# Loading the second pieces of w1 and w2 through two queues, with a new order for the opening of a fused attention and two-layer product kernel

## The chip, the cores and the metric

The kernel runs on one core of a Trainium2 chip. The metric is the device time of one execution in microseconds (us), the median of several runs. Engines are named as in the profile: PE (TensorE matmul), PEld (its weight loads), DVE (VectorE), ACT (ScalarE), POOL (GpSimd) and SP (SyncE, which here only issues transfers).

## What is computed

Three stages follow each other: attention inside chunks of 64 positions, then a gated product, then a product with a cosine gate.

```python
scores = scale * np.matmul(q_c, k_c.transpose(0, 1, 2, 4, 3))   # 8 x 8 heads, 9 chunks of 64
attn = softmax(scores)
x = (attn @ v_c) as [4608, 512]
h = (x @ w1) * (x @ w2) @ w3          # w1, w2: 512 x 1024, w3: 1024 x 1024
x = h @ w_o                           # 1024 x 512
h = x @ w_in                          # 512 x 2048
out = (h * np.cos(h)) @ w_out         # 2048 x 512
```

All weights arrive as 64-bit floats. q, k and v arrive as 32-bit floats.

## The kernel before

The 4,608 tokens are nine blocks of 512, each of four tiles of 128. For each block: four tiles of attention (`attention`, L699 on), a split of the result into two 16-bit parts (`combined`, L643 on), the products with w1 and w2 (`ab`, seven products in place of eight per 2 x 2 quarter, L975), and the product with w3 @ w_o (`u_of`, L1085 to L1087), stored to HBM. Later each block goes through w_in (`h_of`, L1269) and w_out (`y_of`, L1351 to L1353).

Before block 0 can be multiplied, the opening prepares the weights. Each 64-bit weight piece is scaled on ACT and put together from its two 32-bit words on DVE: L602, then L609, L613, L617 (`decode`, for the 8 pieces of w_o and the 16 of w3), or L833, then L836, L839, L842 (`w12_columns`, for w1 and w2). The product w3 @ w_o is computed on PE in 32 bits (`w3_row`: transposes L915, products L923; a product of the program is two recorded matmuls).

w1 and w2 are treated in two column groups each, in the order w1 group 0, w2 group 0, w1 group 1, w2 group 1 (`w12_columns(g, j)`). Each such set has two pieces of 1 MB, 128 partitions by 8 KB. The first piece (b = 0) is one transfer of all 128 partitions (L815). The second piece (b = 1) is wanted with its halves of the partitions exchanged, so it is two transfers of 512 KB, each to 64 partitions (L818, in a loop over `h`). Then follow, for each set: the squares on ACT (L562), column sums by a product with ones on PE (L850), a column maximum (L853) and a short chain of one-column operations on DVE (L537 to L556), four subtractions (L871), and seven pairs of a high part on ACT (L879) and a low part on DVE (L882). The pieces lie in five places of 8 KB in a region called WG (`raw0_p`), so the first five pieces have a place from the start and the last three must wait until an earlier set is done.

Nothing is issued in the order in which it is written. Each step is recorded with `op(engine, cost, priority, ...)`, and `Plan.order` lays the steps out on a model of the five engines: it starts, on each engine that is free, the step with the lowest priority number whose inputs are there by the model. Transfers are modelled as one stream of `DMA_RATE` bytes per us, where a tile of q, k or v counts `ROWS` times its bytes. Each engine then executes its own steps strictly in that order, so an engine whose next step waits holds up all that stands behind it. The priorities of the opening come from constants at L293: `R0, R1` (rows of w3), `C0, C1` (sets of w1 and w2), `A0, A1` (lead and step of the attention of block 0) and `A2, A3` (the same for the later blocks).

```python
for kk in range(K1):
    w3_row(kk, R0 + R1 * kk)
for g in range(2):
    for j in range(2):
        w12_columns(g, j, C0 + 2 * C1 * g + C1 * j)
...
begin, lead, step = start_ab[bl], (A0, A2)[min(bl, 1)], (A1, A3)[min(bl, 1)]
```

SP issues all transfers. Its transfers take turns on eight semaphores, and each waits until the one eight before it has landed, so at most eight are under way; a second piece of w1 or w2 takes two of the eight.

Of the kernel before, what the change touches and what calls it, by code (L numbers as in the profile page):

```python
# [19 lines left out]
P = 128  # L20
# [5 lines left out]

MM = 0.2155
LAT = {"PE": 0.35, "DVE": 0.4, "ACT": 0.4, "POOL": 0.5, "SP": 2.2}
DMA_RATE = 380e3
ROWS = 2.7  # L30
AHEAD = 5.0
SHARED = 0.8
ISSUE = {"DVE": 0.9, "ACT": 0.88}
# [31 lines left out]
class Plan:  # L65
# [50 lines left out]
    def order(self):  # L116
# [26 lines left out]
        now, done, wakes, order, on_psum = 0.0, 0, [0.0], [], False  # L143
# [12 lines left out]
        while done < len(ops):  # L156
# [3 lines left out]
            now = heapq.heappop(wakes)  # L160
# [7 lines left out]
            for e in ENGINES:  # L168
# [9 lines left out]
                while waiting[e]:  # L178
                    x = heapq.heappop(waiting[e])
                    o, taken, where = ops[x[1]], [], []  # L180
# [19 lines left out]
                if got is None:  # L200
                    continue
                o = got
                o.start, o.eng, o.cost = now, e, o.alts[e]
                if e == "DVE":
                    if not o.psum:
                        o.cost += SHARED * max(0.0, free["POOL"] - now)
# [6 lines left out]
                if o.size:  # L213
                    dma = max(dma, now + o.cost) + o.size / DMA_RATE
                    end = dma
# [18 lines left out]
    def emit(self, split):  # L234

        order = self.order()
        last = {}
        for n, o in enumerate(order):
            for b in o.bufs:
                if b.pool is not None:  # L240
                    for x in b.pool.places:
                        if x[0] == "PS" and x[2] == 2 and b.pool.places[b.place] == x:
                            last[x[1]] = n
        then = {n: i for i, n in last.items()}
        for n, o in enumerate(order):
            o.fn(o.eng) if o.many else o.fn()
            if n in then:
                split(then[n])
        return order
# [6 lines left out]
def fused_kernel(  # L256
# [19 lines left out]
    nc = tc.nc  # L276
    B, H, S, D = q.shape
    NT, DM = out.shape
    F1 = w1.shape[1]
    F2 = w_in.shape[1]  # L280
    CH = 64
# [8 lines left out]
    scale = 1.0 / math.sqrt(D)  # L290
    KB = 1024

    R0, R1, C0, C1, A0, A1, A2, A3, I0, I1, I2, I3, I4, I5, F0, F1, Y0 = 0.9, 10.9, 16.5, 27.6, 60.0, 6, 70.0, 10.6, 240.5, 10.0, 28.1, 510.5, 5.6, 11.6, 8.4, -26.5, 55.8  # L293

    const = ctx.enter_context(tc.tile_pool(name="const", bufs=1))
    sb = ctx.enter_context(tc.tile_pool(name="sb", bufs=1))
# [5 lines left out]
    op = plan.op  # L302
# [134 lines left out]
    at = 95.0  # L437
# [5 lines left out]
    at = start_ab[NB - 1] + 4 * group  # L443
# [9 lines left out]
    with tc.manual_schedule():  # L453
# [168 lines left out]
        def block_of(bl, prio, step):  # L622

            for j in range(TPB):
                i = bl * TPB + j
                vt = vts[i] = Buf(v_p, f"v{i}")
                def f(i=i, vt=vt):
                    dst = vt.ap.rearrange("p (c h d) -> p c h d", c=2, h=HP)
                    for c in range(2):
                        bb, s = divmod(i * P + c * CH, S)  # L630
                        for h2 in range(2):
                            nc.sync.dma_start(
                                dst[h2 * CH : (h2 + 1) * CH, c], v[bb, h2::2, s : s + CH, :].rearrange("h p d -> p h d")
                            )
                op("SP", 2.4, prio + step * j - 8, f, w=[vt], size=ROWS * P * 2 * KB)
            xf[bl] = Buf(xf_p, f"xf{bl}")
# [62 lines left out]
        def attention(i, prio):  # L699
# [5 lines left out]
            for src, b in ((q, qt), (k, kt)):  # L705
                def f(src=src, b=b):
                    dst = b.ap.rearrange("p (h d) -> p h d", h=H)
                    for off, n, bb, s in runs:
                        nc.sync.dma_start(dst[off : off + n], src[bb, :, s : s + n, :].rearrange("h p d -> p h d"))
                op("SP", 0.6, prio - 12, f, w=[b], size=ROWS * P * 2 * KB)  # L710
            qkT = []
# [89 lines left out]
        def w12_columns(g, j, prio):  # L801
# [5 lines left out]
            w = (w1, w2)[j].bitcast(U32)[:, cols].rearrange("(c b p) n -> b p c n", c=2, b=2)  # L807
            for b in range(2):
                raw = raws[b] = Buf(raw0_p, f"raww{j}{g}{b}")
                at = prio + b  # L810

                def f(raw=raw, w=w, b=b):
                    dst = raw.ap.rearrange("p (c n) -> p c n", c=2)
                    if b == 0:
                        nc.sync.dma_start(dst, w[0])  # L815
                    else:
                        for h in range(2):
                            nc.sync.dma_start(dst[h * CH : (h + 1) * CH], w[1, (1 - h) * CH : (2 - h) * CH])  # L818
                op("SP", 0.6 * (1 + b), at - 14, f, w=[raw], size=P * 8 * KB)
            cs = Buf(ps_mm, f"pscs{j}{g}")  # L820
            for b in range(2):
                raw, at = raws[b], prio + b
# [9 lines left out]
                def f(high=high):  # L832
                    nc.scalar.activation(high().bitcast(F32), high().bitcast(F32), AF.Copy, scale=2.0**-112)  # L833
                op("ACT", 1.1, at - 2, f, r=[raw], w=[raw])
                def f(high=high, whole=whole):
                    nc.vector.tensor_scalar(whole(), high(), 3, None, ALU.logical_shift_left)  # L836
                op("DVE", 0.75, at, f, r=[raw], w=keys)
                def f(low=low, whole=whole):
                    nc.vector.scalar_tensor_tensor(whole(), low(), 29, whole(), ALU.logical_shift_right, ALU.bitwise_or)  # L839
# [28 lines left out]
            at = prio + 3  # L868
# [505 lines left out]
# [3 lines that stand above are left out]
# [56 lines left out]
```

## Time and profile before

| | |
|---|---|
| median of 3 runs | 1452.89 us (1451.71 to 1454.46) |
| the profiled execution | 1456.48 us |
| its span, first to last instruction | 1454.7 us |
| PE busy in it | 1413.4 us (97%) |
| DVE, ACT, POOL busy | 992.3, 997.8, 347.1 us |
| mean granted TensorE clock | 0.988 of full speed |

The profiled execution took 1.8 us more than its span, and 3.6 us more than the median of the runs. Busy shares are means over the whole program; the opening is read apart from the rest. PEclk is the granted clock of PE as a share of full speed. The idle time beside an instruction is that of its engine just before it, with what ended it.

### The profile page before, as it was taken

How to read it: one execution, taken by the hardware profiler on the slowest of the kernel's cores; microseconds unless marked ns; L12 is line 12 of the kernel's file. 1: busy time of each engine (PE TensorE's matmuls, PEld its weight loads, DVE VectorE, ACT ScalarE, POOL GpSimd, SP SyncE). 2: the span in 40 equal slices, each digit the busy share in tenths (PEclk: the TensorE clock that was granted, in tenths of full speed). 3: DMA queues.
4: the chain of work that ended last, by engine and by line, in shares of the span. 5: the costliest groups of instructions: out<-in, count | busy, mean ns of one | idle time of the engine just before them, and what ended most of it. 6: DMA issues, size and time to landing. Idle time of an engine off the chain costs nothing.

```text
span 1454.7 us, 28969 instructions
## 1 busy us (share of the span) xinstructions
PE 1413.4 (97%) x11683; PEld 979.5 (67%) x11688; DVE 992.3 (68%) x1587; ACT 997.8 (69%) x2152; POOL 347.1 (24%) x250
## 2 busy tenths in 40 slices
PE   5789999999999999999999999999999999999998
PEld 4346768777777768686876777666666666666644
DVE  8779788468997654578589888757485756454510
ACT  5688777678887676697488888667585756574610
POOL 0000014122653111124145342313141322122100
PEclk8989999999999999999999999999999999999999
DMA  9951383227679222275534443333151333333000
GB/s 313 266 116 44 105 292 84 65 68 221 192 224 264 66 60 66 66 216 180 193 106 174 156 160 144 138 116 145 67 194 67 145 109 117 116 116 116 16 22 29
DMA packets 170454, 194.81 MB, mean 134 GB/s; under 512 B 118992, under 2 KB 133328, under 8 KB 169168
## 3 DMA queue, kind: packets, MB, share of 16 engines
q1 hardware_dynamic: 170320, 192.97, 41.8%
q8 instruction: 91, 1.49, 0.4%
q14 instruction: 43, 0.35, 0.1%
HBM read 162.53 MB, written 30.41 MB: 133 GB/s over the span
## 4 chain that ended last, share of the span: by engine, by line
PE 87%; DVE 5%; ACT 4%; DMA 3%; issue 1%; POOL 0%; ACTq 0%; POOLq 0%; SPq 0%
PE ps L1269 21%; PE ps L975 20%; PE ps L1353 8%; PE ps L1351 8%; PE ps L1352 8%; PE ps L1085 4%; PE ps L1086 4%; PE ps L1087 4%; PE ps L923 2%; PE ps L716 2%; PE ps L779 1%; PE ps L731 1%; DMA u_dram<-TMP 1%; PE ps L764 1%; ACT ATT L748 1%
## 5 line engine op out<-in xcount | busy, mean ns | idle before, releaser
L975 PE MATMUL ps<-XHL,W 128*128 128x256 f16 x3024 | 348.9, 273 | 4.9 <-ACT RES L482 4.7
L1269 PEld LDWEIGHTS <-ATT 128*128 128x128 f16 x3024 | 295.7, 98 | 61.2 <-issue 2.3
L975 PEld LDWEIGHTS <-W 128*128 128x128 f16 x3024 | 293.1, 98 | 45.0 <-issue 5.9
L1312 POOL TENSOR_TENSOR W<-W,RES 128x512 f32<-128x512 f32 x105 | 149.6, 1432 | 411.5 <-ACT RES L1309 405.6
L1278 ACT ACTIVATE W<-ps,smalls 128x512 f32<-128x512 f32 x144 | 97.8, 679 | 114.4 <-PE ps L1269 113.9
L1269 PE MATMUL ps<-XHL,ATT 128*128 128x256 f16 x1392 | 167.8, 273 | 1.1 <-ACT W L1278 0.9
L1284 DVE SCALAR_TENSOR_TENSOR W<-ps,smalls,W 128x512 f32<-128x512 f32 x108 | 80.2, 746 | 101.8 <-PE ps L1269 67.4
L482 ACT ACTIVATE RES<-ps,smalls 128x512 f32<-128x512 f32 x126 | 87.1, 697 | 62.8 <-PE ps L975 58.8
L1300 DVE SCALAR_TENSOR_TENSOR RES<-RES,W 128x512 f32<-128x512 f32 x144 | 109.9, 768 | 22.4 <-ACT RES L1296 21.0
L1010 POOL TENSOR_TENSOR WG<-RES,WG 128x512 f16<-128x512 f32 x44 | 58.0, 1324 | 270.6 <-DMA ATT<-in_v_dram 157.5
L1351 PE MATMUL ps<-CONV,W 128*128 128x512 f16 x320 | 121.4, 379 | 0.0
L1353 PE MATMUL ps<-CONV,W 128*128 128x512 f16 x320 | 121.4, 379 | 0.0
L1352 PE MATMUL ps<-CONV,W 128*128 128x512 f16 x320 | 121.4, 379 | 0.0
L1296 ACT ACTIVATE RES<-W,magic 128x512 f32<-128x512 f32 x144 | 102.5, 716 | 27.1 <-DVE W L1284 25.1
L1309 ACT ACTIVATE RES<-RES,half_pi 128x512 f32<-128x512 f32 x144 | 102.6, 715 | 15.1 <-DVE RES L1306 13.8
L995 DVE SCALAR_TENSOR_TENSOR RES<-ps,smalls,RES 128x512 f32<-128x512 f32 x108 | 79.8, 744 | 45.8 <-ACT RES L482 26.8
L1085 PE MATMUL ps<-WG 128*128 128x512 f16 x288 | 109.4, 380 | 0.0
L1086 PE MATMUL ps<-WG 128*128 128x512 f16 x288 | 109.3, 379 | 0.0
L1087 PE MATMUL ps<-WG 128*128 128x512 f16 x288 | 109.3, 379 | 0.0
L748 ACT ACTIVATE ATT<-ps,SMALL 128x64 f32<-128x64 f32 x288 | 85.8, 327 | 21.4 <-DVE SMALL L743 21.4
L1351 PE MATMUL ps<-CONV,WG 128*128 128x512 f16 x256 | 97.2, 380 | 0.0
L1352 PE MATMUL ps<-CONV,WG 128*128 128x512 f16 x256 | 97.1, 379 | 0.0
(186 smaller groups left out, 2504.9 us busy)
## 6 DMA issues: line engine op xcount, KB each, us to landing
ATT<-win_dram SPq DMA_DIRECT2D x72, 896.0 KB, 5.9
CONV<-in_moe_w_in_dram SPq DMA_DIRECT2D x32, 512.0 KB, 6.8
CONV<-in_moe_w_out_dram SPq DMA_DIRECT2D x32, 512.0 KB, 6.7
ATT<-in_v_dram SPq DMA_DIRECT2D x144, 64.0 KB, 2.5
u_dram<-TMP SPq DMA_DIRECT2D x36, 256.0 KB, 2.7
XHL<-u_dram SPq DMA_DIRECT2D x9, 1024.0 KB, 5.4
out_dram<-TMP SPq DMA_DIRECT2D x36, 256.0 KB, 2.0
ATT<-in_q_dram SPq DMA_DIRECT2D x32, 256.0 KB, 3.7
```

The source lines that it names most:

```text
L975: nc.tensor.matmul(ps.ap[:, p * half : (p + 1) * half], w12[j, g].ap[:, b, w_, c, p * P : (p + 1) * P], t[a].ap[:, c, u_], start=(not more ...
L1085: nc.tensor.matmul(ps.ap, wh.ap[:, kk, 0, ns], g[:, 0], start=(kk == 0), stop=False)
L1086: nc.tensor.matmul(ps.ap, wh.ap[:, kk, 0, ns], g[:, 1], start=False, stop=False)
L1087: nc.tensor.matmul(ps.ap, wh.ap[:, kk, 1, ns], g[:, 0], start=False, stop=(kk == K1 - 1))
L1269: nc.tensor.matmul(ps.ap[:, p * half : (p + 1) * half], wins[p].ap[:, b, k, w_], t[a].ap[:, k, u_], start=(not more and p == 0 and k == 0 ...
L1296: nc.scalar.activation(r.ap, hs.ap, AF.Identity, bias=magic)
L1300: nc.vector.scalar_tensor_tensor(r.ap, r.ap, -MAGIC, hs.ap, ALU.add, ALU.subtract)
L1309: nc.scalar.activation(r.ap, r.ap, AF.Sin, bias=half_pi, scale=-2.0 * math.pi)
L1312: engines[eng].tensor_tensor(out=hs.ap, in0=hs.ap, in1=r.ap, op=ALU.mult)
L1351: nc.tensor.matmul(ps.ap, tg.ap[:, kk, 0, js], wout.ap[:, kk, 0], start=(kk == 0), stop=False)
L1352: nc.tensor.matmul(ps.ap, tg.ap[:, kk, 0, js], wout.ap[:, kk, 1], start=False, stop=False)
L1353: nc.tensor.matmul(ps.ap, tg.ap[:, kk, 1, js], wout.ap[:, kk, 0], start=False, stop=(kk == K2 - 1))
```

## The change

The second piece of each set is still two transfers of 64 partitions, but SP issues the one for partitions 0 to 63 and POOL the one for partitions 64 to 127. SP's modelled cost of it is that of one issue. Nine constants of the opening's priorities are new, and so are two of the three that model transfers; a third, COLD, makes PE's steps 1.15 times as long in the first 120 us of the model.

```diff
-DMA_RATE = 380e3
-ROWS = 2.7
+DMA_RATE = 390e3
+ROWS = 2.4
+COLD = 1.15
...
-                o.start, o.eng, o.cost = now, e, o.alts[e]
+                o.start, o.eng, o.cost = now, e, o.alts[e] * (COLD if e == "PE" and now < 120.0 else 1.0)
...
-    R0, R1, C0, C1, A0, A1, A2, A3, I0, I1, I2, I3, I4, I5, F0, F1, Y0 = 0.9, 10.9, 16.5, 27.6, 60.0, 6, 70.0, 10.6, 240.5, 10.0, 28.1, 510.5, 5.6, 11.6, 8.4, -26.5, 55.8
+    R0, R1, C0, C1, A0, A1, A2, A3, I0, I1, I2, I3, I4, I5, F0, F1, Y0 = -3.6, 11.6, 8.2, 26.1, 68.9, 12.1, 76.2, 11.3, 240.5, 10.0, 28.1, 510.5, 5.6, 11.6, 8.4, -26.5, 55.8
...
-                        for h in range(2):
-                            nc.sync.dma_start(dst[h * CH : (h + 1) * CH], w[1, (1 - h) * CH : (2 - h) * CH])
-                op("SP", 0.6 * (1 + b), at - 14, f, w=[raw], size=P * 8 * KB)
+                        nc.sync.dma_start(dst[:CH], w[1, CH:])
+                        nc.gpsimd.dma_start(dst[CH:], w[1, :CH])
+                op("SP", 0.6, at - 14, f, w=[raw], size=P * 8 * KB)
```

The changed program has one line more ahead of all that matters here, so L815 of before is L816 now, L882 is L883, and so on.

Three places of the order. First POOL's own queue, from its first instruction of the kernel's body on. Before:

```order
masks.py:197 MEMSET ident_90 128x128
masks.py:199 ISA
masks.py:199 AFFINE_SELECT ident_90<-ident_90 128x128
L457 MEMSET half_pi_95 128x1
L460 MEMSET magic_97 128x1
L1010 TENSOR_TENSOR WG_68<-RES_70,WG_68 128x2x256 x4
```

Now:

```order
masks.py:197 MEMSET ident_90 128x128
masks.py:199 ISA
masks.py:199 AFFINE_SELECT ident_90<-ident_90 128x128
L458 MEMSET half_pi_95 128x1
L461 MEMSET magic_97 128x1
L819 DMA WG_68<-in_moe_w1_dram 64x2x1024
L819 DMA WG_68<-in_moe_w2_dram 64x2x1024
L819 DMA WG_68<-in_moe_w1_dram 64x2x1024
L819 DMA WG_68<-in_moe_w2_dram 64x2x1024
L1011 TENSOR_TENSOR WG_68<-RES_70,WG_68 128x2x256 x5
```

The four halves stand together at the head of POOL's queue. The first two go into places that are free from the start and wait for nothing; the third and fourth wait for DVE to be done with an earlier set.

Second, SP's queue around the first piece of w1's group 1 (the third set). RES, XHL and W12 are places of w3 pieces, ATT those of q, k, v. Before:

```order
L598 DMA XHL_72<-in_moe_w3_dram 128x1024
L709 DMA ATT_71<-in_q_dram 128x8x64
L709 DMA ATT_71<-in_k_dram 128x8x64
L815 DMA WG_68<-in_moe_w2_dram 128x2x1024
L598 DMA XHL_72<-in_moe_w3_dram 128x1024
L818 DMA WG_68<-in_moe_w2_dram 64x2x1024 x2
L632 DMA ATT_71<-in_v_dram 64x4x64 x4
L598 DMA XHL_72<-in_moe_w3_dram 128x1024
L598 DMA W12_67<-in_moe_w3_dram 128x1024 x3
L815 DMA WG_68<-in_moe_w1_dram 128x2x1024
L818 DMA WG_68<-in_moe_w1_dram 64x2x1024 x2
L598 DMA W12_67<-in_moe_w3_dram 128x1024 x2
```

Now:

```order
L816 DMA WG_68<-in_moe_w2_dram 128x2x1024
L818 DMA WG_68<-in_moe_w2_dram 64x2x1024
L710 DMA ATT_71<-in_q_dram 128x8x64
L710 DMA ATT_71<-in_k_dram 128x8x64
L599 DMA XHL_72<-in_moe_w3_dram 128x1024 x2
L633 DMA ATT_71<-in_v_dram 64x4x64 x4
L599 DMA XHL_72<-in_moe_w3_dram 128x1024
L599 DMA W12_67<-in_moe_w3_dram 128x1024
L816 DMA WG_68<-in_moe_w1_dram 128x2x1024
L599 DMA W12_67<-in_moe_w3_dram 128x1024 x2
L818 DMA WG_68<-in_moe_w1_dram 64x2x1024
```

Counted from the start of the queue, 14 pieces of w3 stood ahead of that first piece before, and 12 do now; two w3 pieces now stand between it and its set's second piece.

Third, DVE's queue up to the first low part of block 0's operands (L659 before, L660 now). Before:

```order
L836 TENSOR_SCALAR W12_67<-WG_68 128x1024
L839 SCALAR_TENSOR_TENSOR W12_67<-WG_68,W12_67 128x1024
L537 TENSOR_REDUCE smalls_87<-ps_3_76 128x1
L539 TENSOR_SCALAR smalls_87<-smalls_87 128x1
L553 TENSOR_SCALAR smalls_87<-smalls_87 128x1
L554 TENSOR_SCALAR smalls_87<-smalls_87 128x1
L555 TENSOR_SCALAR smalls_87<-smalls_87 128x1
L556 TENSOR_SCALAR smalls_87<-smalls_87 128x1
L663 TENSOR_TENSOR RES_70<-XHL_72 128x512
L871 TENSOR_TENSOR WG_68<-WG_68 128x512 x2
L663 TENSOR_TENSOR XHL_72<-XHL_72 128x2x256
L659 SCALAR_TENSOR_TENSOR XHL_72<-XHL_72,smalls_87 128x2x256
```

Now:

```order
L883 SCALAR_TENSOR_TENSOR W12_67<-WG_68,smalls_87,W12_67 128x512 x7
L538 TENSOR_REDUCE smalls_87<-ps_3_76 128x1
L540 TENSOR_SCALAR smalls_87<-smalls_87 128x1
L554 TENSOR_SCALAR smalls_87<-smalls_87 128x1
L555 TENSOR_SCALAR smalls_87<-smalls_87 128x1
L556 TENSOR_SCALAR smalls_87<-smalls_87 128x1
L557 TENSOR_SCALAR smalls_87<-smalls_87 128x1
L664 TENSOR_TENSOR RES_70<-XHL_72 128x512
L664 TENSOR_TENSOR XHL_72<-XHL_72 128x2x256
L872 TENSOR_TENSOR WG_68<-WG_68 128x512
L570 SCALAR_TENSOR_TENSOR smalls_87<-smalls_87 128x1
L660 SCALAR_TENSOR_TENSOR XHL_72<-XHL_72,smalls_87 128x2x256
```

The seven low parts of the third set stood behind that point and stand ahead of it now. Counted over the whole queue, what is ahead of it grows by 7 of L882, 1 of L842, 2 of L871, 1 of L853 and one chain of six one-column operations. On PE, what is ahead of the first product of `ab` grows by 4 products of L923 (60 in place of 56), 4 transposes of L915, 4 products with ones (L850) and one sum.

## Rows read from the trace of the kernel before

**Rows 1.** Busy time by stretch: us, each engine (instructions), PEclk, DMA share, GB/s.

```profile
0.00:180.00 180.00, 146.79 (x1138) 97.06 (x1144) 144.66 (x277) 129.80 (x321) 3.50 (x10) 0.91 0.61 166
180.00:1400.00 1220.00, 1215.74 (x10313) 859.56 (x10312) 847.64 (x1311) 864.59 (x1827) 343.65 (x240) 1.00 0.41 134
```

**Rows 2.** The same view for four stretches of the opening.

```profile
0.00:62.08 62.08, 41.12 (x150) 24.62 (x152) 53.20 (x88) 36.89 (x63) 0.78 (x8) 0.87 1.00 304
62.08:94.60 32.52, 25.89 (x225) 15.15 (x226) 18.24 (x39) 24.02 (x71) 0.00 (x0) 0.77 0.56 136
94.60:118.80 24.20, 21.24 (x168) 11.81 (x168) 23.31 (x41) 19.53 (x63) 0.00 (x0) 1.00 0.55 104
118.80:172.50 53.70, 51.45 (x531) 41.40 (x530) 43.57 (x103) 42.99 (x116) 1.16 (x1) 0.97 0.18 41
```

**Rows 3.** Timeline, 54 to 73 us: start, us, engine and work, [idle before].

```profile
54.04 1.25 SPq L818 DMA_DIRECT2D WG<-in_moe_w_dram  x2
...
64.43 1.15 ACT L833 ACTIVATE WG<-WG 128x1024 f32<-128x1024 f32 x1 [1.81 <-DMA WG<-in_moe_w_dram]
69.41 1.13 ACT L833 ACTIVATE WG<-WG 128x1024 f32<-128x1024 f32 x1 [2.79 <-DMA WG<-in_moe_w_dram]
...
72.93 0.17 DVE L755 TENSOR_SCALAR SMALL<-SMALL 128x8 f32<-128x8 f32 x1 [5.18 <-ACT ATT L748]
```

**Rows 4.** Timeline, start of the program: POOL, ACT and DVE.

```profile
1.28 0.10 POOL L460 MEMSET magic<- 128x1 f32 x1
...
4.41 0.67 ACT L602 ACTIVATE RES<-RES 128x512 f32<-128x512 f32 x1 [2.40 <-DMA RES<-in_moe_w_out_dram]
7.61 0.69 ACT L602 ACTIVATE RES<-RES 128x512 f32<-128x512 f32 x1 [1.24 <-DMA RES<-in_moe_w_out_dram]
8.88 0.67 ACT L602 ACTIVATE XHL<-XHL 128x512 f32<-128x512 f32 x1 [0.58 <-DMA XHL<-in_moe_w_out_dram]
...
8.70 0.42 DVE L609 TENSOR_SCALAR CONV<-RES 128x512 uint32<-128x512 uint32 x1
10.49 0.42 DVE L609 TENSOR_SCALAR CONV<-XHL 128x512 uint32<-128x512 uint32 x1
```

**Rows 5.** Groups by line, DVE, 0 to 180 us: busy us, mean ns, idle.

```profile
L871 DVE TENSOR_TENSOR WG<-WG 128x512 f32<-128x512 f32 x16 | 10.6, 686 | 0.1
L842 DVE SCALAR_TENSOR_TENSOR WG<-WG,W 128x1024 uint32<-128x1024 uint32 x8 | 9.8, 1223 | 0.2
L853 DVE TENSOR_REDUCE smalls<-ps 128x1 f32<-128x512 f32 x4 | 2.7, 684 | 0.0
L553 DVE TENSOR_SCALAR smalls<-smalls 128x1 uint32<-128x1 uint32 x6 | 0.9, 154 | 0.2
```

**Rows 6.** Timeline, work of the kinds that the change moves, DVE and PE.

```profile
122.83 4.72 DVE L882 SCALAR_TENSOR_TENSOR W<-WG,smalls,W 128x512 f16<-128x512 f32 x7
...
102.64 3.60 PE L923 MATMUL ps<-CONV,RES 128*128 128x512 f32 x8
117.76 0.59 PE L850 MATMUL ps<-TMP,ones 128*128 128x512 bf16 x2
118.33 0.64 PE L915 MATMUL ps<-ident,TMP 128*128 128x128 f32 x4
```

**Rows 7.** Timeline, where block 0's products start, and a later wait of PE.

```profile
118.80 1.47 PE L975 MATMUL ps<-XHL,W 128*128 128x256 f16 x12
...
117.91 0.75 DVE L659 SCALAR_TENSOR_TENSOR XHL<-XHL,smalls 128x512 f16<-128x512 f32 x1
...
145.62 2.72 PE L975 MATMUL ps<-XHL,W 128*128 128x256 f16 x12 [2.15 <-ACT RES L482]
```

**Rows 8.** Timeline, the last piece of w2: buffer freed, issue, arrival.

```profile
89.81 2.08 DVE L882 SCALAR_TENSOR_TENSOR W<-WG,smalls,W 128x512 f16<-128x512 f32 x3 [0.30 <-ACT W L879]
...
96.19 1.25 SPq L818 DMA_DIRECT2D WG<-in_moe_w_dram  x2
...
105.23 1.18 ACT L833 ACTIVATE WG<-WG 128x1024 f32<-128x1024 f32 x1 [2.64 <-DMA WG<-in_moe_w_dram]
```

## The prediction

> **What bounds the kernel now.** I read the busy time by stretch first. From 180 to 1400 us PE is busy 1215.74 of 1220 us at the full granted clock [rows 1]: the body is PE at work, it has 4.3 us of idle time, and the change takes no product away. So the change can only pay in the opening, where PE is idle 33.2 of the first 180 us [rows 1]. The stretches say who holds it up there [rows 2]. Up to 62 us DVE is busy 53.20 of 62.08 us and PE 41.12: DVE, which puts the weights together, is the bound. From 62 to 95 us DVE works only 18.24 of 32.52 us and PE is granted 0.77 of its clock: both wait. From 95 to 119 us DVE is full again (23.31 of 24.20). From 119 us on PE is, with 2.25 us idle in 53.7.
>
> The timeline names the largest hole [rows 3]. ACT takes its steps in order, and the two pieces of w1's group 1 stand ahead of the first tile's exponentials. ACT waits for the first piece until 64.43 and for the second until 69.41 us; the exponentials come after it, and DVE, which divides by their sums, idles 5.18 us until 72.93. The second piece was issued only at 54.04, as two halves.
>
> The same rows show why halves are dear. From the first piece's arrival to the second's it takes 69.41 - 64.43 = 4.98 us for 1 MB, two transfers of 64 partitions [rows 3]. At the start, 512 KB over all 128 partitions come every 8.88 - 7.61 = 1.27 us [rows 4], so 1 MB in 2.54. The same bytes in rows of the same 4 KB take twice as long on half of the partitions.
>
> The place where opening and body meet: DVE starts the first low part of block 0's operands at 117.91 us, and PE starts the first of the block's products at 118.80 [rows 7]. From there on PE has enough work. So what counts is when that point comes, less the PE work already done by then.
>
> **The change, part by part**, positive for slower.
>
> *1. Work moved ahead of that point: +3.5 us.* DVE does more before it: seven L882 in a row, 4.72 us [rows 6]; one L842, 1.22; two L871, 1.37; one L853, 0.68; six one-column operations of 0.15, 0.90 [rows 5]: 8.9 us. PE also does more before it, which it need not do later: 3.60 for the products of L923, 0.64 for four transposes, 2 x 0.59 for four products with ones [rows 6]: 5.4 us (one small sum is left out). DVE is the bound up to that point, so the start comes 8.9 later with 5.4 more done: 3.5 lost. It can't be much else, as both counts come from the order.
>
> *2. POOL's first two halves: +1.6 us, between 0 and +4.6.* They wait for nothing, and POOL is through with its constants at 1.38 us [rows 4], so 1 MB is asked for while w_o's first pieces are on their way. SP's own halves go out where they stood, tens of us later for the second set, so these two pairs do not run together. 1 MB at the pace of the rows is 2.54 us. I let it land beside the third and fourth piece, since POOL asks after SP's first loads. The fourth then lands at 8.88 + 2.54 = 11.42, is scaled by 12.09 (0.67 for the scaling), and DVE, which began it at 10.49, is 1.6 us late; later pieces have more room. At best POOL's transfers move after w_o's: 0. At worst they take the 4.98 us of two halves and the third piece waits for all of it: 7.61 + 4.98 + 0.69 = 13.28 against DVE's start at 8.70 [rows 4], 4.6 late.
>
> *3. The hole at 64 to 73 us: -4.1 us, between -5.2 and -1.6.* Two w3 pieces fewer stand ahead of w1's group 1: its first piece comes 2 x 1.27 = 2.5 us earlier. Its second now has two w3 pieces ahead (2.5) and one half on SP's queue (2.5, half of 4.98) where it had two (4.98): also 2.5 earlier. ACT and DVE come 1.6 later (term 2). Of DVE's 5.18, 5.2 - 2.5 - 1.6 = 1.1 is left. Below, the hole closes; above, the transfer comes no earlier and only the 1.6 is saved. Next late is then ACT itself, with the exponentials.
>
> *4. DVE's other waits from 62 to 95 us: -2.0 us, between -9.1 and +5.2.* They are 32.52 - 18.24 - 5.18 = 9.1 us [rows 2, 3], many short ones on ACT and PE in the attention of the first tiles. Every engine's order is new there, and no row shows the new meetings. They can all go (-9.1), or one more hole like the largest can open (+5.2 [rows 3]). No row is nearer to one end, so I take the middle, -2.0.
>
> *5. After the point, and in the body: 0, between -4 and +4.* PE's 2.15 us wait at 145.62 on ACT [rows 7] comes while ACT makes seven high parts in a row; in the new order seven still stand between two of its releases from PSUM, now those of the last set. The body's orders change with A2 and A3; its idle time is 4.3 us [rows 1] and PE hides the rest. I give each about 2 us to either side.
>
> POOL's four issues cost nothing: POOL has nothing else before the block's products. If that cover were gone, its first product step would wait behind the fourth half. SP saves four issues and four of its places among eight; that is inside term 3.
>
> **Sum:** 3.5 + 1.6 - 4.1 - 2.0 + 0 = -1.0 us. The profiled execution took 1456.48 us, 3.6 above the median of the runs; I take the difference over to the median: 1452.89 - 1.0 = 1451.9 us. 0.2% is 2.9 us, about what a measurement of this kernel tells from no change.
>
> The Trainium skill, SBUF — State Buffer, section "Can I just issue two DMAs to hit both halves?", speaks against the change: transfers to partitions from 0 and from 64 are said to serialize, with 6% gained by running them together, whichever engine issues them. The 4.98 us for two halves on one queue agrees with it [rows 3], and no run here shows two queues yet. It is the second rival below.
>
> **Rivals.**
> *Faster: the waits of 62 to 95 us give way.* If the two halves move together on two queues, the third set comes in time, the hole closes (-5.2), half of DVE's other waits go (-4.6), and with the last set done sooner PE's 2.15 us wait goes too (-2.2). Sum 3.5 + 1.6 - 5.2 - 4.6 - 2.2 = -6.9: 1446.0 us. For it: the idle time is there, and 8.9 us of the moved DVE work depends on no attention, so it can fill holes. Against it: in an in-order queue it fills them only where the order happens to put it, and the first two pairs don't run together.
>
> *Serial halves.* A pair takes 4.98 us whatever queue it is on. By the skill's rule above this is what happens. Then the second piece of w1's group 1 has two w3 pieces ahead and a full 4.98 behind them, lands at 69.4 as before, and term 3 is only -1.6: 3.5 + 1.6 - 1.6 - 2.0 = +1.5, 1454.4 us.
>
> *Slower: a new wait at w2's last piece.* On ACT it now stands right after the second tile's exponentials and ahead of the third's. Its place comes free when the second set's low parts end, 89.81 + 2.08 = 91.9 us; SP issued it only at 96.19, 4.3 us later, and it landed at 105.23 [rows 8]. If SP's half is again 4.3 us behind, ACT stands still for that long with the exponentials, PE's transposes and DVE's divisions behind it: -1.0 + 4.3 = +3.3, 1456.2 us, and more if term 2 goes to its end. It decides once that half lands after ACT is done with the second tile's exponentials. Before, ACT's wait there was 2.64 us.
>
> **Chances.** My forecast 0.40, of which 0.30 lies within 0.2% and 0.05 on each side; faster rival 0.32; serial halves 0.10 (0.08 within, 0.02 slower); new wait 0.18. So faster 0.37, same 0.38, slower 0.25. The faster rival reaches to 1445, and the slower one, with term 2 at +4.6 in place of +1.6, to 1459; I take 1445 to 1459.
>
> **What would show it.** In the new profile: POOL's two first halves issued near 1.4 us and ACT's scaling of the fourth w_o piece near 11.4 (term 2); ACT's wait for w1's second piece of group 1 ending near 67 us and DVE's idle before its first division near 1 us (term 3); DVE busy over 18 of the 32 us from 62 on (term 4); the first product of `ab` near 118.8 + 8.9 + 1.6 - 4.1 - 2.0 = 123 us (term 1). The forecast is wrong if that product starts before 119 us or after 127, or if PE's idle time from 180 us on differs from 4.3 us by more than 2.

## The result, and the profile after

| | before | after |
|---|---|---|
| median of 6 runs | 1452.99 us (1451.71 to 1454.46) | 1463.84 us (1461.21 to 1465.21) |
| the profiled execution | 1456.48 us | 1465.21 us |
| its span | 1454.7 us | 1463.4 us |
| PE busy, idle in the span | 1413.4, 41.3 us | 1416.3, 47.1 us |

The change makes the kernel slower: the ratio after to before is 1.0071, 95% interval 1.0058 to 1.0084, or 10.9 us between the medians. 1451.9 us was forecast, and the range ended at 1459. The two traces are of single executions, 3.5 and 1.4 us above these medians, so their spans are 8.7 us apart and not 10.9.

The busy time by stretch of the changed kernel has the same columns as [rows 1]: us, each engine (instructions), PEclk, DMA share, GB/s.

```profile
120.00:140.00 20.00, 15.68 (x83) 8.34 (x83) 18.38 (x48) 14.98 (x28) 0.00 (x0) 0.83 0.06 13
...
0.00:180.00 180.00, 141.91 (x1094) 93.05 (x1100) 139.48 (x271) 126.91 (x316) 5.61 (x14) 0.90 0.57 155
180.00:1400.00 1220.00, 1214.98 (x10317) 859.97 (x10316) 852.45 (x1304) 872.18 (x1838) 353.19 (x246) 1.00 0.42 135
```

The body has 5.0 us of idle PE against 4.3 [rows 1]. In the opening PE idles 38.1 us against 33.2, and from 120 to 140 us, where it was busy 19.90 of 20 us in the kernel before, it works 15.68 at 0.83 of its clock.

The timeline of the changed kernel's start answers to [rows 4]:

```profile
1.53 1.35 POOL L819 DMA_DIRECT2D WG<-in_moe_w_dram  x2
...
5.70 0.69 ACT L603 ACTIVATE RES<-RES 128x512 f32<-128x512 f32 x1 [0.61 <-DMA RES<-in_moe_w_out_dram]
10.60 0.67 ACT L603 ACTIVATE RES<-RES 128x512 f32<-128x512 f32 x1 [4.21 <-DMA RES<-in_moe_w_out_dram]
14.75 0.67 ACT L603 ACTIVATE XHL<-XHL 128x512 f32<-128x512 f32 x1 [3.48 <-DMA XHL<-in_moe_w_out_dram]
...
15.45 0.43 DVE L610 TENSOR_SCALAR CONV<-XHL 128x512 uint32<-128x512 uint32 x1 [2.27 <-ACT XHL L603]
```

POOL's first two halves hold back the third and fourth piece of w_o. DVE begins the fourth at 15.45 in place of 10.49: 5.0 us late.

The timeline at w1's group 1 and the first tile answers to [rows 3]:

```profile
60.98 1.16 ACT L834 ACTIVATE WG<-WG 128x1024 f32<-128x1024 f32 x1 [0.82 <-DMA WG<-in_moe_w_dram]
68.31 1.15 ACT L834 ACTIVATE WG<-WG 128x1024 f32<-128x1024 f32 x1 [1.59 <-DMA WG<-in_moe_w_dram]
69.35 0.30 ACT L749 ACTIVATE ATT<-ps,SMALL 128x64 f32<-128x64 f32 x1
...
71.83 0.17 DVE L756 TENSOR_SCALAR SMALL<-SMALL 128x8 f32<-128x8 f32 x1 [2.81 <-ACT ATT L749]
...
72.88 6.75 PE L924 MATMUL ps<-CONV,RES 128*128 128x512 f32 x8 [3.83 <-ACT RES L479]
80.80 0.69 PE L780 MATMUL ps<-ATT 64*64 64x64 f32 x32 [0.29 <-ACT ATT L479]
```

The same place before:

```profile
74.50 1.12 PE L764 MATMUL ps<-ident,ATT 128*128 128x128 f32 x4 [4.36 <-ACT ATT L478]
77.65 1.13 PE L779 MATMUL ps<-ATT 64*64 64x64 f32 x32
...
79.16 6.13 PE L923 MATMUL ps<-CONV,RES 128*128 128x512 f32 x8
```

The first piece comes 3.45 us earlier than before, the second 1.1. DVE's wait before the first division shrinks from 5.18 to 2.81 us. But on PE eight products of w3 (L924) now stand ahead of the first tile's transposes, and the copy on ACT (L479) that they need stands behind the exponentials. PE waits 3.83 us for it (4.36 before, for the transposes' own copy), and the eight products take 6.75 us at 0.54 of the clock, where such a group takes 3.60 at the full clock [rows 6]. So the first tile's P times V (the product of its probabilities with v) comes at 80.80, and before at 77.65, where the eight products followed it. A low clock there is not new: before, they took 6.13 us.

The timeline from the second tile to the first product of `ab` answers to [rows 7, 8]:

```profile
93.00 1.14 ACT L834 ACTIVATE WG<-WG 128x1024 f32<-128x1024 f32 x1 [2.66 <-DMA WG<-in_moe_w_dram]
...
98.22 0.43 DVE L610 TENSOR_SCALAR RES<-W 128x512 uint32<-128x512 uint32 x1 [7.32 <-PE ps L916]
...
124.35 0.69 PE L780 MATMUL ps<-ATT 64*64 64x64 f32 x32 [2.03 <-ACT ATT L479]
127.79 1.11 PE L916 MATMUL ps<-ident,TMP 128*128 128x128 f32 x4 [2.15 <-DVE smalls L538]
128.99 6.01 PE L924 MATMUL ps<-CONV,RES 128*128 128x512 f32 x8
135.40 1.47 PE L976 MATMUL ps<-XHL,W 128*128 128x256 f16 x12
...
130.53 0.75 DVE L660 SCALAR_TENSOR_TENSOR XHL<-XHL,smalls 128x512 f16<-128x512 f32 x1
```

DVE has a new hole of 7.32 us. Its first low part of block 0 comes at 130.53 (117.91 before), the first product at 135.40 (118.80 before): 16.6 us later, with 5.4 us more of PE's work done, so 11.2 us are lost by then. That is more than the 8.7 us between the spans: after it the changed kernel gains. Busy time by stretch from there on, before and then now:

```profile
118.80:180.00 61.20, 58.55 (x600) 45.49 (x599) 49.91 (x111) 49.36 (x128) 2.72 (x2) 0.97 0.27 68
```

```profile
140.00:160.00 20.00, 20.00 (x241) 17.48 (x243) 14.41 (x38) 16.94 (x55) 1.16 (x1) 1.00 0.24 54
```

Before, PE idled 2.65 us between the first product of `ab` and 180 us. Now it does not wait at all there. DVE's busy time up to its first low part, in both kernels (the rows of before have 53.12 us up to 62), tells how the 12.6 us on DVE came:

```profile
62.00:117.91 55.91, 46.32 (x384) 26.17 (x386) 40.77 (x79) 42.79 (x131) 0.00 (x0) 0.86 0.56 125
```

```profile
0.00:62.00 62.00, 39.94 (x138) 24.05 (x140) 49.96 (x83) 34.03 (x56) 2.71 (x11) 0.83 1.02 294
...
62.00:130.53 68.53, 52.55 (x410) 29.08 (x413) 51.91 (x102) 52.28 (x150) 0.58 (x1) 0.90 0.43 110
```

DVE works 101.87 us in place of 93.89 (8.0 more), idles 12.04 in place of 8.88 up to 62 us (3.2 more), and 16.62 in place of 15.14 after it (1.5 more).

### The profile page after: what moved, and what is told of

It reads as the page before. It is cut to its first block, busy times and chain, and to the rows that moved or that the text cites. A ratio compares the mean times of both kernels' runs of the same rounds, so it can differ in the third digit from the quotient of the medians.

```text
span 1463.4 us, 28969 instructions
## 1 busy us (share of the span) xinstructions
PE 1416.3 (97%) x11683; PEld 979.7 (67%) x11688; DVE 991.9 (68%) x1574; ACT 1003.2 (69%) x2159; POOL 358.8 (25%) x260
## 4 chain that ended last, share of the span: by engine, by line
PE 84%; DMA 8%; DVE 4%; ACT 3%; issue 1%; SPq 0%; ACTq 0%; DVEq 0%
PE ps L1270 22%; PE ps L976 19%; PE ps L1354 8%; PE ps L1353 8%; PE ps L1352 8%; PE ps L1086 4%; PE ps L1088 4%; PE ps L1087 4%; DMA WG<-in_moe_w_dram 3%; DMA CONV<-in_moe_w_out_dram 2%; PE ps L924 2%; PE ps L717 2%; PE ps L780 1%; PE ps L732 1%; DMA XHL<-in_moe_w_out_dram 1%; DMA CONV<-in_moe_w_in_dram 1%
## 5 line engine op out<-in xcount | busy, mean ns | idle before, releaser
L1313 POOL TENSOR_TENSOR W<-W,RES 128x512 f32<-128x512 f32 x109 | 157.2, 1449 | 440.8 <-ACT RES L1310 420.5
L1270 PE MATMUL ps<-XHL,ATT 128*128 128x256 f16 x1344 | 162.3, 273 | 1.9 <-DMA ATT<-win_dram 1.6
L1011 POOL TENSOR_TENSOR WG<-RES,WG 128x512 f16<-128x512 f32 x50 | 63.7, 1277 | 285.8 <-ACT WG L479 285.6
L1301 DVE SCALAR_TENSOR_TENSOR RES<-RES,W 128x512 f32<-128x512 f32 x144 | 113.9, 795 | 22.6 <-ACT RES L1297 21.9
```

The costliest lines, as they stand in the source:

```text
L1270: nc.tensor.matmul(ps.ap[:, p * half : (p + 1) * half], wins[p].ap[:, b, k, w_], t[a].ap[:, k, u_], start=(not more and p == 0 and k == 0 ...
L1301: nc.vector.scalar_tensor_tensor(r.ap, r.ap, -MAGIC, hs.ap, ALU.add, ALU.subtract)
L1313: engines[eng].tensor_tensor(out=hs.ap, in0=hs.ap, in1=r.ap, op=ALU.mult)
```

## The experiments

The ratio of each run is to the kernel before on the same chip, with its 95% interval; 0.001 is 1.45 us. The changed kernel stands at 1.0071.

**Is it the split of the loads?** Four kernels: the changed one with all halves on SP (e1), the old order with POOL's halves (e2), the changed one with group 0's halves on SP (e3), and one that makes POOL wait for an earlier piece (e4). PE, DVE and ACT keep their order in all.

```diff
 e1:
-                        nc.gpsimd.dma_start(dst[CH:], w[1, :CH])
+                        nc.sync.dma_start(dst[CH:], w[1, :CH])
 e2, in the kernel before:
-                        for h in range(2):
-                            nc.sync.dma_start(dst[h * CH : (h + 1) * CH], w[1, (1 - h) * CH : (2 - h) * CH])
+                        nc.sync.dma_start(dst[:CH], w[1, CH:])
+                        nc.gpsimd.dma_start(dst[CH:], w[1, :CH])
 e3:
+                        (nc.gpsimd if g else nc.sync).dma_start(dst[CH:], w[1, :CH])
 e4, ahead of POOL's transfer (loaded: the pieces of w_o and w3 that SP has asked for so far):
+                        if g == 0:
+                            nc.gpsimd.tensor_copy(tiny, loaded[-4].ap[:, 0, 0:1])
```

> The changed kernel with POOL's halves put back on SP's queue; PE, DVE and ACT keep the changed kernel's order. Theory A (POOL's two early halves hold back w_o by 5 us and that is carried to the end, the other 6 us are the new order's): the fourth w_o piece is scaled near 9 us again instead of 14.75, the first product of ab starts 3 to 5 us before 135.4, and the time is 1458 to 1460 us. Rival B (the order alone makes all of it, the late start is taken up by later waits): 1463 to 1465 us. Rival C (the two queues alone make all of it): 1452 to 1454 us.

> The kernel before with only the split: second halves on POOL, order of PE, DVE and ACT untouched. Theory A: DVE's first steps come 5 us later, the hole at 64 to 73 us shrinks by 2 to 3, the time is 1455 to 1458 us. Rival B (order alone): 1450 to 1454 us. Rival C (queues alone): 1462 to 1465 us.

> The changed kernel, but the two early halves (group 0) back on SP, the two late ones (group 1) still on POOL. Theory A: the w_o pieces come as in the kernel before, 1457 to 1459 us, no more than 2 us quicker than with all on SP. Rival B: 1463 to 1465. Rival C': if the late pairs on two queues are what costs, this stays at 1463 or more while all on SP is quicker.

> The changed kernel with all four halves on POOL, but POOL's first two held until an earlier piece of SP's queue has landed (POOL copies one word of it per partition), so that they run beside SP's halves. Theory A: as group 0 on SP, 1457 to 1459 us, and the first pair lands in under 4 us if two queues move two halves together, in about 5 if they take turns. Rival B: 1463 to 1465 us.

Measured: e1 1462.12 us, 1.0055 (1.0042 to 1.0068); e2 1452.88, 1.0001 (0.9991 to 1.0011); e3 1465.01, 1.0079 (1.0064 to 1.0094); e4 1464.94, 1.0074 (1.0060 to 1.0088). Rival B holds in the main: the order makes the loss, and in the old order the split costs nothing. In e2 the fourth piece is scaled at 14.80, as late as in the changed kernel, and `ab` still starts at 115.40. The 5 us are real and are taken up by later waits. In e4 the early pairs did not run side by side after all: POOL's halves went out at 16.05 and 28.70 us, SP's at 11.54 and 33.05.

One thing is left over. With all halves on SP, e1 is 2.9 us quicker than e3, as rival C' has it (the late pairs on two queues cost). Their traces don't show that as its cause: in e3 the late pieces of w1 and w2 come no later (67.69 and 91.36 us, against 68.02 and 92.24 in e1), and `ab` starts 0.4 us earlier. The difference of their spans is idle time of PE from 180 to 1400 us (6.28 against 3.28 us), where no half is loaded. In e4 that idle time is 9.6 us, and there `ab` starts 5.0 us earlier than in the changed kernel without any gain. So in this order the body can take back what the opening gives; why stays open.

What the two queues do to a pair was to be seen at w2's last piece. Timeline of e1, both halves on SP, then of the changed kernel:

```profile
84.02 0.61 SPq L818 DMA_DIRECT2D WG<-in_moe_w_dram  x1
84.67 0.62 SPq L819 DMA_DIRECT2D WG<-in_moe_w_dram  x1
...
92.24 1.10 ACT L834 ACTIVATE WG<-WG 128x1024 f32<-128x1024 f32 x1 [3.58 <-DMA WG<-in_moe_w_dram]
```

```profile
85.71 0.59 SPq L818 DMA_DIRECT2D WG<-in_moe_w_dram  x1
...
85.98 0.58 POOL L819 DMA_DIRECT2D WG<-in_moe_w_dram  x1 [30.50 <-DMA ATT<-in_v_dram]
```

From the first issue to ACT's start it is 8.2 us on one queue and 7.3 on two. But the other eight kernels that issue this pair on two queues within 0.3 us, and in which ACT waits for it, need 6.9 (e4) to 8.4 us (v7). For the pair before it, w1's of group 1, 13.7 us pass on one queue (e1) and on two (e3, the changed kernel). No gain of the second queue shows. The Trainium skill, SBUF — State Buffer, section "Can I just issue two DMAs to hit both halves?", says that transfers to the two halves of the partitions serialize and gives 6% for running them together. These pairs agree with it: a gain of that size would lie within what they scatter.

**Is it DVE's hole and the work moved ahead?** The runs named v and b7 leave the plan as it is and move single steps of it (by their number) ahead of another step, each behind all that it reads. PE's order is untouched in all.

```diff
 v2 (plan.own is 2 KB of RES, unused there, for the w3 piece of L610 at 98.22):
+    order = shifted(order, [295, 297, 299, 302, 311], 294)
+    for b in {id(b): b for o in order for b in o.bufs if b.name == "w3_7_0"}.values():
+        b.pool, b.place = plan.own, 0
 v3:
+    order = shifted(order, [381, 383], 366)
 v4:
+    order = shifted(order, [361, 364, 368, 370, 373, 377, 379], 421)
 v5: the lines of v4, then those of v2
 v6 (v4, and ACT's seven high parts):
+    order = shifted(order, [357, 358, 360, 363, 369, 372, 375, 361, 364, 368, 370, 373, 377, 379], 421)
```

> The changed kernel, but the w3 piece whose decoding DVE waits 7.32 us for gets its own 2 KB, and five DVE steps of w1's group 1 (5.5 us) go ahead of the third tile's maximum, so that the hole at 91 to 98 us is filled. Theory D (all of the loss is ahead of the first product of ab, and DVE's hole there is on its path): DVE comes to its first low part 4.5 to 5.5 us earlier than 130.5, ab starts 4 to 5 us before 135.4, the time is 1458 to 1460 us. Rival E (PE and ACT hold the opening up anyway, the hole only moves): 1462 to 1465 us.

> The changed kernel, but DVE reads the small sums (PE's bank) after two of the seven low parts of L883 instead of after all seven. The theory on the join: PE's wait of 2.15 us at 127.79 goes, its eight products of L924 run before DVE is done with block 0's first low part, ab starts near 131.4 in place of 135.4, and the time is 1459 to 1461 us. Rival: these products must be made anyway and PE only waits later, 1463 to 1465 us.

> The changed kernel, but the seven low parts of w1's group 1 (4.72 us of DVE) stand after block 0's low parts instead of ahead of them, as they did in the kernel before. Theory (work moved ahead of the point is paid in full): DVE's first low part of block 0 near 125.8, ab near 130.3 instead of 135.4, 1458 to 1460 us. Rival (PE is the bound at the join, or the seven are waited for afterwards): over 1462 us.

> Both edits of v2 and v4. If hole and moved work are separate causes, the gains add: 9 to 10 us, 1453 to 1455 us, about the kernel before. If they are one cause seen twice: 1458 to 1460 us.

> As v4, and ACT's seven high parts of w1's group 1 go behind block 0's operands too, so that ACT's copy of the fourth tile's transposed probabilities no longer stands behind four of them. Theory F (the fourth tile's attention, through ACT, sets when ab starts, not DVE's work): that copy at 121 to 122 us in place of 124.06, P times V at 122 to 123 in place of 124.68, ab at 128 to 131 in place of 135.1, and 1461 to 1465 us, 4 to 8 below v4. Rival (PE's own queue of w3 products sets it): ab stays at 134 to 136 and the time above 1466.

Measured: v2 1465.55 us, 1.0093 (1.0076 to 1.0109); v3 1462.50, 1.0075 (1.0060 to 1.0089); v4 1469.37, 1.0115 (1.0093 to 1.0138); v5 1466.41, 1.0102 (1.0085 to 1.0119); v6 1464.95, 1.0093 (1.0080 to 1.0106). None is faster than the changed kernel. My theory D and that of the join fell. Busy time by stretch and timeline of v2, then PE at the join in v3:

```profile
100.00:120.00 20.00, 18.85 (x129) 10.27 (x126) 13.41 (x24) 14.73 (x54) 0.00 (x0) 1.00 0.28 64
```

```profile
135.26 1.47 PE L976 MATMUL ps<-XHL,W 128*128 128x256 f16 x12
```

```profile
128.89 5.48 PE L924 MATMUL ps<-CONV,RES 128*128 128x512 f32 x8 [2.73 <-ACT RES L479]
```

The hole is filled (DVE is busy 29.37 us from 62 to 100, against 22.96), and DVE then idles from 100 on instead: 13.41 busy against 18.80. `ab` starts where it did. In v3 PE's wait for DVE at the join is gone, and it waits for ACT's copy in its place, so that the eight products start at 128.89 where they started at 128.99. So DVE is not what bounds this stretch in the new order; the tiles' attention on PE and ACT is. In v6, where ACT's high parts moved too, the product that opens `ab` did come 6.4 us earlier, as theory F has it: 7.8 us after the fourth tile's P times V, in place of 11.1. PE then waited 3.58 us for a small sum behind the seven parts that had been moved, and the time shows no gain:

```profile
128.96 1.47 PE L976 MATMUL ps<-XHL,W 128*128 128x256 f16 x12
...
139.37 0.90 PE L717 MATMUL ps<-ident,ATT 128*128 128x128 f32 x3 [3.58 <-DVE smalls L538]
```

**Which constants?** Three plans made anew, and r3's with e3's line. (Eight of the opening's priorities changed, R0 to A3; the nine told above were a miscount.)

```diff
 r8, changed kernel:  A1 = 12.1 -> 6
 r2, kernel before:   A0, A1 = 60.0, 6 -> 68.9, 12.1
 r3, changed kernel:  DMA_RATE = 390e3 -> 380e3, ROWS = 2.4 -> 2.7, COLD = 1.15 -> 1.0
 s3:                  r3, with e3's line
```

> The changed kernel with one constant set back: A1, the step between the priorities of block 0's four tiles, 6 in place of 12.1; the order is planned anew. Theory F: the fourth tile's P times V comes over 8 us earlier than 124.35, ab starts at 120 to 126, the time is 1453 to 1458 us. Rival (the sets' and w3's priorities or the rates make it): ab stays above 130 and the time above 1461.

> The kernel before with only A0 and A1 of the change (68.9 and 12.1): the four tiles of block 0 spread out, all else old, halves on SP. Theory F: the fourth tile's P times V 6 us or more later than 111.56, ab later than 118.8 by 3 to 8 us, 1455 to 1460 us. Rival: no change, 1451 to 1454.

> The changed kernel with the planner's old rates (380e3, rows at 2.7, no dearer cold products), new priorities kept. If the priorities make the loss: 1459 to 1466 us. If the rates do: 1451 to 1455 us.

> The kernel with the old rates and new priorities, with the two early halves on SP's queue again. If the 5 us by which the early halves hold back w_o are carried to the end in this order: 1447 to 1449 us. If they are taken up by later waits, as in the old and the changed order: 1450 to 1453 us.

Measured: r8 1457.92 us, 1.0051 (1.0037 to 1.0065); r2 1451.48, 0.9997 (0.9986 to 1.0009); r3 1452.18, 1.0004 (0.9995 to 1.0013); s3 1451.50, 0.9996 (0.9986 to 1.0006). With the new priorities and the split, but the old rates, the loss is gone: 0.0067, or 9.7 us, hang on the three numbers with which the planner models transfers and early products. Which of them stays open: no plan with one alone was run. With the old step of the tiles under the new rates (r8), `ab` starts at 122.40 and some 3 us come back, though the intervals of r8 and the changed kernel overlap by a little. Its plan also has the exponentials ahead of w1's second scaling, so the step's own share isn't told apart. In the old order the new step costs nothing (r2), so it isn't the cause by itself.

Timeline of r3, first tile and start of `ab`, and its body:

```profile
64.92 0.31 ACT L749 ACTIVATE ATT<-ps,SMALL 128x64 f32<-128x64 f32 x1 [0.18 <-DVE SMALL L744]
...
67.25 0.62 ACT L479 COPY RES<-ps 128x512 f32<-128x512 f32 x1
67.72 1.21 ACT L834 ACTIVATE WG<-WG 128x1024 f32<-128x1024 f32 x1
...
67.92 3.70 PE L924 MATMUL ps<-CONV,RES 128*128 128x512 f32 x8 [1.15 <-ACT RES L479]
73.38 0.69 PE L780 MATMUL ps<-ATT 64*64 64x64 f32 x32 [0.89 <-ACT ATT L479]
128.46 1.47 PE L976 MATMUL ps<-XHL,W 128*128 128x256 f16 x12
```

```profile
180.00:1400.00 1220.00, 1218.47 (x10295) 860.42 (x10293) 846.09 (x1305) 862.71 (x1821) 350.72 (x245) 1.00 0.41 135
```

Here the exponentials and the copy behind them stand ahead of the two scalings. ACT does them while the loads are under way, PE waits 1.15 us in place of 3.83 and keeps its clock, and the first tile's P times V comes at 73.38, not 80.80. That lead of 7.4 us is 6.9 at the first product of `ab`. 3.5 us more come in the body (1.5 us of idle PE against 5.0; kernels with the changed kernel's order have 3.2 to 9.6 us there). PE's own order is not the cause: up to `ab`, r3 and the changed kernel have the same 558 recorded matmuls in the same order. What differs ahead of it is the order on DVE, ACT and SP.

**Is it the scalings ahead of the exponentials?** ACT's two scalings moved behind them in the changed kernel (v7) and in the kernel before (b7), ahead of them in r3 (v8).

```diff
 v7:
+    order = shifted(order, [175, 200], 213)
 v8, in r3:
+    order = shifted(order, [202, 208], 190)
 b7, in the kernel before:
+    order = shifted(order, [195, 203], 224)
```

> The changed kernel with one edit in ACT's order alone: its two scalings of w1's group 1, which wait for the loads until 60.98 and 68.31 us, go behind the first tile's exponentials and the copy after them. Theory G (the waits for these loads sit ahead of the first tile's exponentials and hold back every tile after it): the exponentials start at 66 to 67 us in place of 69.35, the first tile's P times V at 74 to 76 in place of 80.80, all later tiles and the first product of ab 4 to 6 us earlier than 135.4, 1457 to 1460 us. Rival (the order behind that place makes the loss): ab within 1.5 us of 135.4 and 1462 to 1465 us.

> The kernel with the old rates and new priorities (r3_old_rates, 1452.2) with the opposite edit: the same two scalings put ahead of the first tile's exponentials, where the changed kernel has them. Theory G: the exponentials start near 70 us in place of 64.92, ab at 132 to 135 in place of 128.46, 1456 to 1459 us. Rival: 1451 to 1454 us.

> The kernel before with the same edit as v7: the two scalings behind the first tile's exponentials and three copies. Theory G: the exponentials start near 66 us in place of 70.44, DVE's wait of 5.18 us goes, and the kernel takes 1448 to 1451 us, less than both kernels. Rival (the wait only moves, as the filled hole did): 1451 to 1454 us.

Measured: v7 1465.35 us, 1.0094 (1.0078 to 1.0111); v8 1457.19, 1.0044 (1.0027 to 1.0061); b7 1450.28, 0.9988 (0.9976 to 1.0000). Put in, the order costs r3 0.0040, 5.8 us, as theory G says. With the 3.5 us of the body (v8's body is r3's, 1.6 us of idle PE) that makes 9.3 of the 9.7 us between r3 and the changed kernel. Taken out of the kernel before, which has the exponentials behind the scalings too, it gives some 2 us, at the edge of the interval. In v8's timeline PE waits 3.91 us again, the first tile's P times V is at 77.06 and `ab` at 131.00:

```profile
70.55 5.35 PE L924 MATMUL ps<-CONV,RES 128*128 128x512 f32 x8 [3.91 <-ACT RES L479]
77.06 0.69 PE L780 MATMUL ps<-ATT 64*64 64x64 f32 x32 [0.29 <-ACT ATT L479]
...
131.00 1.47 PE L976 MATMUL ps<-XHL,W 128*128 128x256 f16 x12
```

But taken out of the changed kernel (v7) it gives nothing. Timeline of v7:

```profile
66.62 0.69 ACT L603 ACTIVATE W<-W 128x512 f32<-128x512 f32 x1 [2.13 <-DMA W<-in_moe_w_dram]
67.20 0.29 ACT L749 ACTIVATE ATT<-ps,SMALL 128x64 f32<-128x64 f32 x1
...
70.94 0.65 ACT L603 ACTIVATE W<-W 128x512 f32<-128x512 f32 x1 [1.29 <-DMA W<-in_moe_w_dram]
...
72.12 5.37 PE L924 MATMUL ps<-CONV,RES 128*128 128x512 f32 x8 [4.68 <-ACT RES L479]
78.65 0.69 PE L780 MATMUL ps<-ATT 64*64 64x64 f32 x32 [0.29 <-ACT ATT L479]
...
135.41 1.47 PE L976 MATMUL ps<-XHL,W 128*128 128x256 f16 x12
```

The exponentials start 2.15 us earlier, but PE gains nothing that can be told from scatter. The nine kernels with ACT's steps in the changed kernel's order up to here (with it, e1, e3, e4 and v2 to v6) have the first tile's P times V at 76.83 to 81.31, v7 has it at 78.65, and v9 and v10, with the same edit, at 80.48 and 81.31. What holds PE now is the next steps in ACT's queue. Scalings of w3 pieces (L603) stand ahead of the exponentials and of the copy that PE needs, and they wait for their own loads, 2.13 and 1.29 us. PE waits 4.68 us for the copy, in place of 3.83. In r3's order no scaling stands between the exponentials and the copy, and those ahead of them did not wait. No run moved these scalings too, so this is read from the traces and not shown by an edit.

**Do the waits stand in series?** v9 is v7 with ACT's scaling of w2's last piece (at 93.00 us in the changed kernel) moved behind the second tile's copies; v10 has, besides, v2's filled hole, and DVE's small sums and ACT's copy of the fourth tile ahead of the high and low parts.

```diff
 v9:
+    order = shifted(order, [271], 289)
+    order = shifted(order, [175, 200], 213)
 v10, v9 and v2's lines, and ahead of them:
+    order = shifted(order, [381, 383], 366)
+    order = shifted(order, [357, 358, 360, 361, 363, 364], 370)
```

> The changed kernel with v7's edit and ACT's scaling of w2's last piece (wait of 2.66 us until 93.00, ahead of the copy of the second tile's transposed probabilities) put behind that tile's copies. Theory H (the waits stand in series, each edit alone only hands its gain to the next wait): the second tile's P times V at 91 to 93 in place of 96.47, ab 2 to 4 us before 135.4, 1459 to 1462 us. Rival (PE's own queue sets the pace from 86 us on): ab within 1 us of 135.4, 1463 to 1466.

> The changed kernel with the edits of v9, the filled hole of v2, and at the join DVE's small sums and ACT's copy of the fourth tile's transposed probabilities ahead of w1's group 1's high and low parts. PE's order is untouched. Theory H: the gains that none of the edits had alone come together, ab at 124 to 129 and 1454 to 1459 us. Rival (PE's order itself, w3's products between the tiles, makes the loss): ab at 131 or later and 1461 us or more.

Measured: v9 1459.32 us, 1.0051 (1.0037 to 1.0065); v10 1463.35, 1.0076 (1.0063 to 1.0090). In v9 the second tile's P times V follows 13.98 us after the first's, where it takes 14.83 to 16.05 in v7 and in the nine kernels with that scaling in its old place (15.67 in the changed one). `ab` is at 132.07, 3.3 us earlier than in the changed kernel, but e1, e3 and e4 have it at 130.38 to 133.30 without the edit:

```profile
80.48 0.69 PE L780 MATMUL ps<-ATT 64*64 64x64 f32 x32 [0.29 <-ACT ATT L479]
94.46 0.69 PE L780 MATMUL ps<-ATT 64*64 64x64 f32 x32 [0.88 <-ACT ATT L479]
...
132.07 1.47 PE L976 MATMUL ps<-XHL,W 128*128 128x256 f16 x12
```

With w1's and w2's scalings out of the tiles' way some 3 us come back (0.0020, though the two intervals overlap by a little) that neither v7 nor any other edit to ACT or DVE had. v10 missed. PE comes earlier to its last eight products before `ab`, but ACT's copy for them still stands behind seven high parts, so PE waits 5.34 us and starts them at 129.11 (128.99 in the changed kernel):

```profile
129.11 6.01 PE L924 MATMUL ps<-CONV,RES 128*128 128x512 f32 x8 [5.34 <-ACT RES L479]
```

So v10 doesn't tell whether all waits together cover the loss. That stays open. Its rival, PE's own order, fits v10's numbers (`ab` at 135.53 us) but falls by r3, which has that order and is as fast as the kernel before.

## Why the prediction was wrong

The view of where it would be decided was right: the body gave 0.7 us more idle time, and the loss arises ahead of the first product of `ab`. By the prediction's own sign, that product starting after 127 us, it was wrong: it starts at 135.40. The terms, as forecast and as they came between the two traces:

| term | forecast | came |
|---|---|---|
| 1, moved work (DVE more, PE's part less) | 8.9 - 5.4 = +3.5 | 8.0 - 5.4 = +2.6 |
| 2, POOL's first halves (DVE's idle time up to 62 us) | +1.6 | +3.2 |
| 3 and 4, DVE's waits from 62 us on | -6.1 | +1.5 |
| from DVE's first low part to `ab`, 0.89 to 4.87 us | none | +4.0 |
| 5, after that point | 0 | -2.5 |
| sum | -1.0 | +8.7 (10.9 by the medians) |

**Term 4 is the step that failed first.** It took the middle between "all waits go" and "one more hole", because no row was nearer to one end, although every engine's order was new. One more hole did open, 7.32 us, longer than the 5.18 on which the upper end was set. With term 3 the sum was off by 7.6 us.

**Term 3 was half right.** The pieces came 3.45 and 1.1 us earlier where 2.5 was forecast for both, and DVE's wait fell to 2.81 us in place of 1.1. What the step left out is what else stands behind those scalings on ACT, the copy that PE's eight products need, and that these products now stand ahead of the first tile's transposes: the first division comes 1.1 us earlier than before, the first tile's P times V 3.15 us later.

**The frame "DVE is the bound up to that point" failed**, and with it the way in which the terms were added. v2, v4 and v5 take DVE's waits and moved work away and gain nothing. The kernel r3 has the same seven low parts ahead of the point, starts `ab` 9.7 us later than before, and is as fast as before. For the same reason the start of `ab` was taken as DVE's first low part plus 0.9 us. In the new order PE has eight products ahead of it that wait for DVE's small sum behind the seven low parts (2.15 us) or, with that wait gone, for ACT's copy (2.73 us in v3), and then run at the lower clock (6.01 us); 4.0 us had no term at all.

**Term 2 was sized too low and mattered little.** 5.0 us at the fourth w_o piece is past the upper end of 4.6, but e1, e3 and e2 show that it is worth 0 to 2.3 us at the end.

**Term 5** kept PE's wait of 2.15 us after the start of `ab`. That wait went (2.65 us less idle time up to 180 us), and the body took 0.7 us back.

**The rivals.** "Slower: a new wait at w2's last piece" named a place that counts, though not its price: the wait is 2.66 us, as before (2.64), and moving the scaling brings the second tile 0.9 us or more closer to the first (v9). "Serial halves" is what the pairs do, as far as these runs tell (6.9 to 8.4 us on two queues, 8.2 on one), and it did not decide: e1 and e2 put the loss on the order. "Faster" saw the idle time of 62 to 95 us rightly as usable: in r3 DVE is busy 30.40 of the 38 us from 62 to 100, against 22.96. It was an order that could use it, and the changed kernel's is not.

The range left out such a loss because the ends of the terms were not taken together: terms 2 and 4 at their upper ends alone would have given 1462.1.

## What to carry to other kernels

In an in-order queue a step that waits for a load should not stand ahead of a short chain that other engines wait for: look, for every new order, at which load waits stand ahead of which releases (v8: 5.8 us). The rates with which a planner models transfers count only through the order that comes out: between r3 and the changed kernel two near-equal sets of rates are 9.7 us apart. Waits in series hide each other, so an edit at one of them that brings nothing does not clear it: look at which step of the same queue waits in its place. And before a lead of 2 us in one trace is called the edit's, look at how far the same step scatters between kernels that don't differ there.

## What was not expected of the hardware

POOL's two halves, asked for at 1.53 us, slowed all loads on their way: from 5.70 to 14.75 us 265 GB/s were moved, where the kernel before moved 396 in the same time with the DMA engines as busy (1.03 and 1.02). Only two of SP's 512 KB pieces came in these 9.0 us, where they come every 1.27 us otherwise. The runs that move only these halves agree: 385 and 395 GB/s with them on SP in the changed order (e1, e3), 256 with them on POOL in the old order (e2). Why the rate falls stays open.

A wait costs PE more than its length. The same group of eight products of L924 takes 3.70 us after a wait of 1.15 us (r3, granted clock 1.00), and 6.75 us after one of 3.83 (0.54), 6.01 after one of 5.34 (v10, 0.61): after the longer waits a part of the group ran at the 1.2 GHz level. The price does not grow with the wait, though: after 4.59 us (e1) the group took 5.40, as after 1.98 (v2). The granted clock of the changed kernel's 20 us around the join is 0.83. Of the 8.7 us between the two spans, 2.9 are more busy time of PE for the same products.
